# Output projection read by heads, softmax sums on TensorE, and the attention moved ahead of the second FFN product in a decode kernel

## The chip, the cores and the metric

The kernel runs on one core of a Trainium2 chip. A core has five engines that run their own instruction streams and wait for each other through semaphores: TensorE (PE: matmuls and the loads of their stationary operand), VectorE (DVE), ScalarE (ACT), GpSimd (POOL) and SyncE (SP), whose queue issues nearly all of this kernel's DMAs. Sixteen DMA engines move data between HBM and SBUF. The metric is the device time of one execution in microseconds (us); lower is better. Times of several executions are given by their median.

## The reference

One token of a decoder layer, with an attention part and an MLP part in parallel, both from the same normalised row:

```python
xn  = layernorm(x)                                   # x: [1, 1, 1024]
# attention: 32 query heads, 4 KV heads, the last 4096 positions of the cache
q   = (xn @ wq).reshape(1, 1, 32, 128).transpose(0, 2, 1, 3)
s   = einsum("bhqd,bhkd->bhqk", q, repeat(k_cache[:, :, -4096:], 8, axis=1)) * 128**-0.5
o   = einsum("bhqk,bhkd->bhqd", softmax(s), repeat(v_cache[:, :, -4096:], 8, axis=1))
A   = o.transpose(0, 2, 1, 3).reshape(1, 1, 4096) @ wo
# MLP
h   = gelu(layernorm(xn) @ w1 + b1)                  # 3584 wide, tanh form
B   = h @ w2 + b2
out = x + A + B
```

All inputs are bf16. With one token, every weight and every cache row is used once: wq and wo have 8.4 MB each, w1 and w2 7.3 MB each, the window of K and of V 4.2 MB each, 39.9 MB together.

## The kernel before

The program is written in blocks, one for each step and engine; each engine runs its blocks in the order in which they are written, with no planner or scheduler behind it. So the order of TensorE's work is the order of its blocks in the source. Every engine has one semaphore that counts its marked instructions, and a block waits for a count of another engine.

**Loads.** SP issues, in this order, wq in 8 chunks of 1 MB (L166), w1 in 8 chunks (L169), K in 4 (L172), V in 4 (L177). Then it waits until TensorE has finished the w1 product, because w2 is loaded over w1, and issues w2 in 4 chunks of 9, 9, 8 and 2 groups (L642), and after a wait for the wq product, whose buffer WA it takes, wo in 9 chunks of 4 or 2 groups (L650). Each chunk has its own semaphore. In all of them a partition receives one contiguous piece of DRAM; for wo, partition p holds rows 32p to 32p+31, 8 KB in a chunk of four.

**First half.** TensorE makes the row of q = xn·wq (L292, 64 matmuls with one column of xn as stationary operand and 512 columns of wq moving) and of h = y·w1 (L319, 56 matmuls), each as a row on one partition. Short transpositions turn q into QT (head dimension on partitions, L332) and h into columns (L371). K is transposed in 8 units of 16 blocks (L441), which DVE and ACT copy back from PSUM (L456, L468). The GELU of h runs on DVE and ACT (L381 to L404) into GT, a column for each group of 128.

**Second half, in TensorE's order.** Scores: 128 matmuls of 128x8 (L484), one for each KV head and block of 128 positions. The maximum for each head is taken on DVE (L494), transposed and spread over partitions by TensorE (L504, L520), and subtracted on DVE (L546); ACT takes the exp into Pb (L555). While DVE and ACT do this, TensorE adds x and b2 into the output row (4 matmuls, L530 and L534) and the first chunk of w2 (18 matmuls, L413). Then come the sums of the softmax: DVE reduces Pb over the blocks (L560, SUMP), TensorE adds over partitions with a column of ones (L568), DVE takes the reciprocal (L574), TensorE spreads it (L579), DVE copies it to RB. P·V is 128 matmuls of 128x8 (L595). DVE multiplies by RB into OT: head dimension on partitions, one column for each head (L606).

**From OT to wo.** With wo's rows at partition p = row // 32, the column that belongs to wo's group j holds the output values 32p + j, which OT has at another place. So OT is transposed (L612), copied (L618), multiplied by four 0/1 matrices that POOL made at the start in EB (L626), and copied to OJ (L635). The rest of w2 follows (38 matmuls, L413), then 64 matmuls of wo (L667) with a column of OJ as stationary operand. All of x, b2, w2 and wo accumulate in one row of PSUM:

```python
pe.wait_ge(s_wo[j], 16)
...
last = pe.matmul(
    PS[0:1, 6 * 512 + n * 512: 6 * 512 + (n + 1) * 512],
    lhsT=OJ[:, jj:jj + 1],
    rhs=WA[:, jj * D + n * 512: jj * D + (n + 1) * 512],
    start=False, stop=(jj == HQ - 1))
```

ACT and DVE copy the halves of the row to SBUF (L678, L684), and SP stores it (L690).

Of the kernel before, what the change touches and what calls it, by code (L numbers as in the profile page):

```python
# [37 lines left out]
def bass_parallel_sum__sliding_block_cached__mixer_channel_mlp__decode_kernel(  # L38
# [60 lines left out]
    DIAG = nc.alloc_sbuf_tensor("DIAG", [32, 32], dt.float32)  # L99
    NMB = nc.alloc_sbuf_tensor("NMB", [128, 32], dt.float32)  # L100
    Pb = nc.alloc_sbuf_tensor("Pb", [128, HKV * NBLK * REP], dt.bfloat16)
    SUMP = nc.alloc_sbuf_tensor("SUMP", [128, 32], dt.float32)
    REC = nc.alloc_sbuf_tensor("REC", [1, 32], dt.float32)
    RB = nc.alloc_sbuf_tensor("RB", [128, 32], dt.float32)
    OT = nc.alloc_sbuf_tensor("OT", [128, HQ], dt.bfloat16)
    KV = nc.alloc_sbuf_tensor("KV", [128, HKV * W + HKV * NBLK * DH], dt.bfloat16)
    KT = KV[:, 0:HKV * W]
    V = KV[:, HKV * W: HKV * W + HKV * NBLK * DH]
    OTt = nc.alloc_sbuf_tensor("OTt", [32, 128], dt.bfloat16)
    EB = nc.alloc_sbuf_tensor("EB", [32, 4 * 128], dt.bfloat16)  # L110
    OJ = nc.alloc_sbuf_tensor("OJ", [128, 32], dt.bfloat16)
    W1 = nc.alloc_sbuf_tensor("W1", [128, KC * F], dt.bfloat16)
    W2 = W1[:, 0:FC * D]
    WA = nc.alloc_sbuf_tensor("WA", [128, KC * NQ], dt.bfloat16)
# [10 lines left out]
    b2_row = B_b2.rearrange("(o n) -> o n", o=1)  # L125
    b1_T = B_b1.rearrange("(p c) -> p c", c=FC)
    w2_pcn = B_w2.rearrange("(p c) n -> p c n", c=FC)
    wo_pjn = A_wo.rearrange("(p j) n -> p j n", j=32)
    out_row = out.rearrange("b s n -> (b s) n")

    STATE = {}
# [1 line left out]
    with nc.Block() as block:  # L133

        @block.gpsimd
        def _(pool):
            with nc.allow_non_contiguous_dma(reason="small loads"):
                pool.dma_start(X8[:, :], x_rows8).then_inc(s_x8, 16)
                pool.dma_start(XBR[:, 0:D], x_row).then_inc(s_xrow, 16)
                pool.dma_start(XBR[:, D:2 * D], b2_row).then_inc(s_b2, 16)  # L140
                pool.dma_start(B1T[:, :], b1_T).then_inc(s_b1T, 16)
            POOL.mark(pool.memset(identb[:, :], 0.0))
            pool.wait_ge(POOL.sem, POOL.cnt)
            STATE["c_identb"] = POOL.mark(pool.affine_select(
                out=identb[:, :], in_=identb[:, :],
                pattern=[[-1, 128]], compare_op=ALU.not_equal, fill=1.0,
                base=0, channel_multiplier=1))
            POOL.mark(pool.memset(identf[:, :], 0.0))
            pool.wait_ge(POOL.sem, POOL.cnt)
            STATE["c_identf"] = POOL.mark(pool.affine_select(  # L150
                out=identf[:, :], in_=identf[:, :],
                pattern=[[-1, 128]], compare_op=ALU.not_equal, fill=1.0,
                base=0, channel_multiplier=1))
            STATE["c_onesf"] = POOL.mark(pool.memset(onesf[:, :], 1.0))
            POOL.mark(pool.memset(EB[:, :], 0.0))
            pool.wait_ge(POOL.sem, POOL.cnt)
            for r in range(4):
                ins = pool.tensor_copy(
                    EB[:, r * 128:(r + 1) * 128].rearrange("h (a b) -> h a b", b=4)[:, :, r],
                    identb[0:32, 0:32])  # L160
            STATE["c_eb"] = POOL.mark(ins)

        @block.sync
        def _(sp):
# [211 lines left out]
        def gelu_sections():  # L376
            @block.vector
            def _(dve):
                dve.wait_ge(PE.sem, STATE["pe_hT"])
                dve.wait_ge(s_b1T, 16)  # L380
                STATE["d_HT"] = DVE.mark(dve.tensor_tensor(  # L381
                    out=HT[:, :], in0=PSb[:, 7 * 1024: 7 * 1024 + 2 * FC: 2], in1=B1T[:, :], op=ALU.add))
                dve.wait_ge(DVE.sem, DVE.cnt)
                DVE.mark(dve.tensor_tensor(out=U2[:, :], in0=HT[:, :], in1=HT[:, :], op=ALU.mult))
                dve.wait_ge(DVE.sem, DVE.cnt)
                DVE.mark(dve.tensor_scalar(out=U2[:, :], in0=U2[:, :], scalar1=0.044715, scalar2=1.0,
                                           op0=ALU.mult, op1=ALU.add))
                dve.wait_ge(DVE.sem, DVE.cnt)
                STATE["d_T"] = DVE.mark(dve.tensor_tensor(out=U2[:, :], in0=U2[:, :], in1=HT[:, :], op=ALU.mult))
# [29 lines left out]
        for u in range(NUNIT):  # L419
            g = u // 2  # L420
            hu = u % 2
            if u == 3:
                hT_section()

            @block.tensor
            def _(pe, u=u, g=g, hu=hu):
# [35 lines left out]
            if use_act:  # L462
                @block.scalar
                def _(act, u=u, g=g, hu=hu):
# [3 lines left out]
                    STATE["a_ktcopy"][u] = ACT.mark(act.activation(  # L468
                        out=KT[:, g * W + (hu * 16 + 8) * 128: g * W + (hu * 16 + 16) * 128],
                        in_=PSb[:, bk * 1024:(bk + 1) * 1024], func=ACTF.Copy))  # L470

        gelu_sections()

        @block.tensor
        def _(pe):
# [44 lines left out]
            STATE["pe_nmb"] = PE.mark(pe.matmul(  # L520
                PS[:, 2 * 512 + 128: 2 * 512 + 160], lhsT=onesf[0:32, :], rhs=DIAG[:, :]))

        @block.tensor
        def _(pe):
            pe.wait_ge(DVE.sem, STATE["d_QT"])
            pe.wait_ge(DVE.sem, STATE["d_HT"])
            pe.wait_ge(s_xrow, 16)
            pe.wait_ge(s_b2, 16)
            for n in range(2):
                pe.matmul(  # L530
                    PS[0:1, 6 * 512 + n * 512: 6 * 512 + (n + 1) * 512],
                    lhsT=identb[0:1, 0:1], rhs=XBR[0:1, n * 512:(n + 1) * 512],
                    start=True, stop=False)
                pe.matmul(  # L534
                    PS[0:1, 6 * 512 + n * 512: 6 * 512 + (n + 1) * 512],
                    lhsT=identb[0:1, 0:1], rhs=XBR[0:1, D + n * 512:D + (n + 1) * 512],
                    start=False, stop=False)
            pe.wait_ge(DVE.sem, STATE["d_GT"])
            w2_chunk_mms(pe, 0)

        @block.vector
        def _(dve):
            dve.wait_ge(PE.sem, STATE["pe_nmb"])
# [10 lines left out]
            act.wait_ge(DVE.sem, STATE["d_se"])  # L554
            STATE["a_exp"] = ACT.mark(act.activation(out=Pb[:, :], in_=PS[:, 0:1024], func=ACTF.Exp, scale=SCALE))  # L555

        @block.vector
        def _(dve):
            dve.wait_ge(ACT.sem, STATE["a_exp"])
            STATE["d_sump"] = DVE.mark(dve.tensor_reduce(  # L560
                out=SUMP[:, :],
                in_=Pb[:, :].rearrange("p (g b h) -> p g h b", g=HKV, b=NBLK, h=REP),
                axis=AX.X, op=ALU.add))

        @block.tensor
        def _(pe):
            pe.wait_ge(DVE.sem, STATE["d_sump"])
            STATE["pe_tot"] = PE.mark(pe.matmul(  # L568
                PS[0:1, 3 * 512: 3 * 512 + 32], lhsT=onesf[:, 0:1], rhs=SUMP[:, :]))

        @block.vector
        def _(dve):
# [33 lines left out]
            STATE["d_OT"] = DVE.mark(dve.tensor_tensor(  # L606
                out=OT[:, :], in0=PS[:, 4 * 512: 4 * 512 + 32], in1=RB[:, :], op=ALU.mult))

        @block.tensor
        def _(pe):  # L610
            pe.wait_ge(DVE.sem, STATE["d_OT"])
            STATE["pe_ott"] = PE.mark(pe.matmul(  # L612
                PSb[0:32, 5 * 1024: 5 * 1024 + 128], lhsT=OT[:, :], rhs=identb[:, :], is_transpose=True))

        @block.vector
        def _(dve):
            dve.wait_ge(PE.sem, STATE["pe_ott"])
            STATE["d_ott"] = DVE.mark(dve.tensor_copy(OTt[:, :], PSb[0:32, 5 * 1024: 5 * 1024 + 128]))  # L618

        @block.tensor  # L620
        def _(pe):
            pe.wait_ge(DVE.sem, STATE["d_ott"])
            pe.wait_ge(POOL.sem, STATE["c_eb"])
            last = None
            for r in range(4):
                last = pe.matmul(  # L626
                    PS[:, 5 * 512 + 128: 5 * 512 + 160],
                    lhsT=EB[:, r * 128:(r + 1) * 128], rhs=OTt[:, r * 32:(r + 1) * 32],
                    start=(r == 0), stop=(r == 3))
            STATE["pe_oj"] = PE.mark(last)  # L630

        @block.vector
        def _(dve):
            dve.wait_ge(PE.sem, STATE["pe_oj"])
            STATE["d_OJ"] = DVE.mark(dve.tensor_copy(OJ[:, :], PS[:, 5 * 512 + 128: 5 * 512 + 160]))  # L635

        @block.sync
        def _(sp):
            sp.wait_ge(PE.sem, STATE["pe_h"])
            c0 = 0  # L640
            for j, nch in enumerate(W2_CHUNKS):
                sp.dma_start(  # L642
                    W2[:, c0 * D:(c0 + nch) * D].rearrange("p (c n) -> p c n", c=nch),
                    w2_pcn[:, c0:c0 + nch, :],
                ).then_inc(s_w2[j], 16)
                c0 += nch
            sp.wait_ge(PE.sem, STATE["pe_q"])
            j0 = 0
            for j, nj in enumerate(WO_CHUNKS):
                sp.dma_start(  # L650
                    WA[:, j0 * D:(j0 + nj) * D].rearrange("p (jj n) -> p jj n", jj=nj),
                    wo_pjn[:, j0:j0 + nj, :],
                ).then_inc(s_wo[j], 16)
                j0 += nj

        @block.tensor
        def _(pe):
            for j in range(1, len(W2_CHUNKS)):
                w2_chunk_mms(pe, j)
            pe.wait_ge(DVE.sem, STATE["d_OJ"])  # L660
            last = None
            jj = 0
            for j, nj in enumerate(WO_CHUNKS):
                pe.wait_ge(s_wo[j], 16)
                for _ in range(nj):
                    for n in range(2):
                        last = pe.matmul(  # L667
                            PS[0:1, 6 * 512 + n * 512: 6 * 512 + (n + 1) * 512],
                            lhsT=OJ[:, jj:jj + 1],
                            rhs=WA[:, jj * D + n * 512: jj * D + (n + 1) * 512],  # L670
                            start=False, stop=(jj == HQ - 1))
                    jj += 1
            STATE["pe_fin"] = PE.mark(last)

        @block.scalar
# [46 lines left out]
```

## Time and profile before

| what | value |
|---|---|
| median of 6 runs | 111.44 us (109.59 to 111.86) |
| profiled execution, its own time | 111.26 us |
| its span in the profile | 109.1 us |
| PE busy, matmuls | 83.6 us (77%), 705 matmuls |
| DVE, ACT, POOL busy | 22.5, 14.2, 4.6 us |
| DMA | 39.95 MB, mean 366 GB/s over the span |
| chain that ended last | DMA of w1 and w2 46%, PE 34%, SP queue 13% |
| w2 matmuls (L413) | 56, mean 482 ns |
| wo matmuls (L667) | 64, mean 379 ns |
| scores (L484), P·V (L595) | 128 each, 3.4 and 3.5 us |

The span runs from the first to the last instruction of the profiled execution; 2.16 us of its time lie outside it. Matmuls are pipelined, so that the mean duration of one is longer than the distance between two; distances come from the starts. "PEclk" is the clock that TensorE was granted, as a share of full speed. The chain is followed back from the last instruction, at each step to what released it; "issue" in it is time in which an engine waited for nothing that the profile shows. Busy time is an average over stages with different limits, so the stage where a change lies has to be read by itself.

### The profile page before, as it was taken

The page shows a single profiled execution, that of the slowest core. Times are in us where ns is not written, and L with a number is a line of the kernel's source. Part 1 is how long each engine was busy: PE and PEld are TensorE (multiplying, and loading weights), DVE is VectorE, ACT ScalarE, POOL GpSimd, SP SyncE. Part 2 cuts the span into 40 slices and gives each one's busy share as a digit, 9 for nine tenths or more (in the row PEclk, how much of TensorE's full clock was granted, in tenths as well). Part 3 has the DMA queues.
Part 4 walks back from the last instruction along what each step waited for, and adds up shares of the span by engine and source line. Part 5 has one row for each costly group of instructions (what it writes and reads, how often), then busy time and mean ns, then how long its engine had stood idle before and what let it go on. Part 6 is the DMA issues. An engine that isn't in the chain of part 4 may idle for free.

```text
span 109.1 us, 1585 instructions
## 1 busy us (share of the span) xinstructions
PE 83.6 (77%) x705; PEld 41.7 (38%) x705; DVE 22.5 (21%) x49; ACT 14.2 (13%) x16; POOL 4.6 (4%) x18
## 2 busy tenths in 40 slices
PE   0022999999299888499989381998818999999991
PEld 0021233432133222399989230236702334334330
DVE  0015300000700000557396567001001000000002
ACT  4000600000600000534473002000000000000002
POOL 6820000000000000000000000000000000000000
PEclk9999999999999999959999555559965599999999
DMA  3999999999999999999999999999999999970000
GB/s 54 415 420 424 430 418 415 424 421 418 421 415 406 418 426 423 415 421 424 418 412 443 425 419 426 418 461 389 413 418 421 406 421 424 413 302 18 0 0 1
DMA packets 5463, 39.95 MB, mean 366 GB/s; under 512 B 721, under 2 KB 721, under 8 KB 2130
## 3 DMA queue, kind: packets, MB, share of 16 engines
q1 hardware_dynamic: 5330, 39.85, 88.6%
q8 instruction: 5, 0.08, 0.3%
q0 software_dynamic: 128, 0.01, 0.1%
HBM read 39.86 MB, written 0.00 MB: 366 GB/s over the span
## 4 chain that ended last, share of the span: by engine, by line
DMA 46%; PE 34%; SPq 13%; issue 3%; DVE 1%
DMA W<-in_B_w_dram 46%; PE PS L413 16%; PE PS L667 13%; SPq L169 9%; SPq L166 4%; PE PS L595 3%; PE PS L319 2%; DVE ROW L684 1%; PE PS L579 0%; DVE REC L574 0%; PE PS L612 0%; PE PS L626 0%; DVE OTt L618 0%; DVE OT L606 0%; PE PS L568 0%
## 5 line engine op out<-in xcount | busy, mean ns | idle before, releaser
L413 PE MATMUL PS<-W,GT 128*1 128x512 bf16 x56 | 17.2, 482 | 2.2 <-DMA W<-in_B_w_dram 2.2
L292 PE MATMUL PS<-WA,XNTb 128*1 128x512 bf16 x64 | 16.0, 416 | 0.3 <-DVE msy L253 0.3
L319 PE MATMUL PS<-W,YTb 128*1 128x512 bf16 x56 | 12.9, 378 | 3.9 <-DVE ROW L302 2.4
L667 PE MATMUL PS<-WA,OJ 128*1 128x512 bf16 x64 | 14.0, 379 | 0.0
L413 PEld LDWEIGHTS PS<-W,GT 128*1 128x1 bf16 x56 | 5.5, 101 | 13.9 <-issue 10.1
L441 PE MATMUL PS<-identb,KV 128*128 128x128 bf16 x128 | 8.9, 240 | 1.5 <-ACT ROW L345 1.5
L292 PEld LDWEIGHTS PS<-WA,XNTb 128*1 128x1 bf16 x64 | 5.7, 90 | 10.2 <-issue 2.9
L441 PEld LDWEIGHTS PS<-identb,KV 128*128 128x128 bf16 x128 | 8.6, 110 | 1.6 <-ACT ROW L345 1.6
L319 PEld LDWEIGHTS PS<-W,YTb 128*1 128x1 bf16 x56 | 4.3, 83 | 12.5 <-DMA W<-in_B_w_dram 3.5
L667 PEld LDWEIGHTS PS<-WA,OJ 128*1 128x1 bf16 x64 | 5.4, 84 | 8.4
L456 DVE COPY KV<-PS 128x1024 bf16<-128x1024 bf16 x10 | 6.5, 687 | 4.0 <-PE PS L441 4.0
L468 ACT ACTIVATE KV<-PS 128x1024 bf16<-128x1024 bf16 x6 | 5.9, 1021 | 5.9 <-PE PS L441 5.9
L678 ACT ACTIVATE ROW<-PS 1x512 bf16<-1x512 f32 x1 | 0.6, 586 | 40.6 <-PE PS L667 40.6
L684 DVE CAST ROW<-PS 1x512 bf16<-1x512 f32 x1 | 0.7, 679 | 24.0 <-PE PS L667 24.0
L595 PE MATMUL PS<-Pb,KV 128*128 128x8 bf16 x128 | 3.5, 166 | 2.6 <-issue 2.6
L302 DVE CAST ROW<-PS 1x2048 bf16<-1x2048 f32 x1 | 2.3, 2279 | 14.8 <-PE PS L292 14.8
L186 PE MATMUL PS<-identb,X 8*128 8x8 bf16 x1 | 0.2, 185 | 6.7 <-DMA X<-in_A_x_dram 6.7
L595 PEld LDWEIGHTS PS<-Pb,KV 128*128 128x128 bf16 x128 | 3.4, 96 | 2.7 <-issue 2.7
L307 ACT ACTIVATE ROW<-PS 1x2048 bf16<-1x2048 f32 x1 | 1.9, 1866 | 13.8 <-PE PS L292 13.8
L484 PE MATMUL PS<-QT,KV 128*128 128x8 bf16 x128 | 3.4, 167 | 0.3 <-ACT KV L468 0.3
L484 PEld LDWEIGHTS PS<-QT,KV 128*128 128x128 bf16 x128 | 3.4, 98 | 0.5 <-DVE KV L456 0.5
L345 ACT ACTIVATE ROW<-PS 1x1536 bf16<-1x1536 f32 x1 | 1.4, 1439 | 15.8 <-PE PS L332 15.8
(84 smaller groups left out, 37.0 us busy)
## 6 DMA issues: line engine op xcount, KB each, us to landing
WA<-in_A_wq_dram SPq DMA_DIRECT2D x8, 1024.0 KB, 12.0
W<-in_B_w_dram SPq DMA_DIRECT2D x8, 896.0 KB, 25.9
WA<-in_A_wo_dram SPq DMA_DIRECT2D x7, 1024.0 KB, 34.6
W<-in_B_w_dram SPq DMA_DIRECT2D x2, 2304.0 KB, 26.3
KV<-in_A_k_cache_dram SPq DMA_DIRECT2D x4, 1024.0 KB, 26.6
KV<-in_A_v_cache_dram SPq DMA_DIRECT2D x4, 1024.0 KB, 27.4
W<-in_B_w_dram SPq DMA_DIRECT2D x1, 2048.0 KB, 33.3
WA<-in_A_wo_dram SPq DMA_DIRECT2D x2, 512.0 KB, 24.3
```

The lines of the kernel that those rows point to most:

```text
L166: sp.dma_start(WA[:, k * NQ:(k + 1) * NQ], A_wq[k * 128:(k + 1) * 128, :]).then_inc(s_wq[k], 16)
L169: sp.dma_start(W1[:, k * F:(k + 1) * F], B_w1[k * 128:(k + 1) * 128, :]).then_inc(s_w1[k], 16)
L292: last = pe.matmul(PS[0:1, n * 512:(n + 1) * 512], lhsT=XNTb[:, k:k + 1], rhs=WA[:, k * NQ + n * 512: k * NQ + (n + 1) * 512], start=(k == ...
L302: STATE["d_qrow0"] = DVE.mark(dve.tensor_copy(Qrow[:, 0:2048], PS[0:1, 0:2048]))
L319: last = pe.matmul(PS[0:1, (n + 1) * 512:(n + 2) * 512], lhsT=YTb[:, k:k + 1], rhs=W1[:, k * F + n * 512: k * F + (n + 1) * 512], start=(k ...
L413: pe.matmul(PS[0:1, 6 * 512 + n * 512: 6 * 512 + (n + 1) * 512], lhsT=GT[:, c:c + 1], rhs=reg[:, n * 512:(n + 1) * 512], start=False, stop ...
L441: last = pe.matmul(PSb[:, col0: col0 + 128], lhsT=KT[:, g * W + b * 128: g * W + (b + 1) * 128], rhs=identb[:, :], is_transpose=True)
L456: last = dve.tensor_copy(KT[:, g * W + (hu * 16 + 8 * s_) * 128: g * W + (hu * 16 + 8 * s_ + 8) * 128], PSb[:, bk * 1024:(bk + 1) * 1024])
L468: STATE["a_ktcopy"][u] = ACT.mark(act.activation(out=KT[:, g * W + (hu * 16 + 8) * 128: g * W + (hu * 16 + 16) * 128], in_=PSb[:, bk * 102 ...
L484: last = pe.matmul(PS[:, bank_base + b * 8: bank_base + (b + 1) * 8], lhsT=KT[:, g * W + b * 128: g * W + (b + 1) * 128], rhs=QT[:, g * 8: ...
L595: last = pe.matmul(PS[:, 4 * 512 + g * REP: 4 * 512 + (g + 1) * REP], lhsT=V[:, (g * NBLK + b) * DH:(g * NBLK + b + 1) * DH], rhs=Pb[:, (g ...
L667: last = pe.matmul(PS[0:1, 6 * 512 + n * 512: 6 * 512 + (n + 1) * 512], lhsT=OJ[:, jj:jj + 1], rhs=WA[:, jj * D + n * 512: jj * D + (n + 1 ...
```

## The change

It changes four things together.

1. wo is loaded by heads: partition d of group h receives row 128h + d, so that the column of OT for head h is the stationary operand as it is. A chunk of four groups is then four rows of 2 KB for each partition. The transposition, the permutation and their buffers (OTt, EB, OJ) go.
2. The sums of the softmax are made by 128 matmuls with a column of bf16 ones as stationary operand, straight from Pb, in place of DVE's reduction and one fp32 matmul.
3. TensorE's order after the maximum is now: sums, broadcast of the reciprocal, P·V, x and b2, all of w2, wo. Before, x, b2 and the first w2 chunk stood ahead of the sums, and the other w2 chunks behind the permutation.
4. The addition of b1 (HT) is written ahead of the fourth transposition unit, and the rest of the GELU behind the exp.

The diff, cut to its core:

```diff
-    POOL.mark(pool.memset(EB[:, :], 0.0))
-    pool.wait_ge(POOL.sem, POOL.cnt)
-    for r in range(4):
-        ins = pool.tensor_copy(
-            EB[:, r * 128:(r + 1) * 128].rearrange("h (a b) -> h a b", b=4)[:, :, r],
-            identb[0:32, 0:32])
-    STATE["c_eb"] = POOL.mark(ins)
+    STATE["c_onesb"] = POOL.mark(pool.memset(ones_b[:, :], 1.0))
...
         STATE["d_HT"] = DVE.mark(dve.tensor_tensor(...op=ALU.add))
-        dve.wait_ge(DVE.sem, DVE.cnt)
+
+def gelu_sections2():
+    @block.vector
+    def _(dve):
+        dve.wait_ge(DVE.sem, STATE["d_HT"])
         DVE.mark(dve.tensor_tensor(out=U2[:, :], in0=HT[:, :], in1=HT[:, :], op=ALU.mult))
...
     if u == 3:
         hT_section()
+        gelu_sections()
...
-gelu_sections()
-
 ...
...
...
-pe.wait_ge(DVE.sem, STATE["d_GT"])
-w2_chunk_mms(pe, 0)
 ...
-dve.wait_ge(ACT.sem, STATE["a_exp"])
-STATE["d_sump"] = DVE.mark(dve.tensor_reduce(
-    out=SUMP[:, :], in_=Pb[:, :].rearrange("p (g b h) -> p g h b", g=HKV, b=NBLK, h=REP),
-    axis=AX.X, op=ALU.add))
-pe.wait_ge(DVE.sem, STATE["d_sump"])
-STATE["pe_tot"] = PE.mark(pe.matmul(
-    PS[0:1, 3 * 512: 3 * 512 + 32], lhsT=onesf[:, 0:1], rhs=SUMP[:, :]))
+gelu_sections2()
+pe.wait_ge(ACT.sem, STATE["a_exp"])
+pe.wait_ge(POOL.sem, STATE["c_onesb"])
+for g in range(HKV):
+    for b in range(NBLK):
+        last = pe.matmul(
+            PS[0:1, 3 * 512 + g * REP: 3 * 512 + (g + 1) * REP],
+            lhsT=ones_b[:, 0:1],
+            rhs=Pb[:, (g * NBLK + b) * REP:(g * NBLK + b + 1) * REP],
+            start=(b == 0), stop=(b == NBLK - 1))
+STATE["pe_tot"] = PE.mark(last)
 ...
...
...
-wo_pjn = A_wo.rearrange("(p j) n -> p j n", j=32)
 for j, nh in enumerate(WO_CHUNKS):
     sp.dma_start(
-        WA[:, j0 * D:(j0 + nj) * D].rearrange("p (jj n) -> p jj n", jj=nj),
-        wo_pjn[:, j0:j0 + nj, :],
+        WA[:, h0 * D:(h0 + nh) * D].rearrange("p (h n) -> p h n", h=nh),
+        A_wo[h0 * 128:(h0 + nh) * 128, :].rearrange("(h d) n -> d h n", h=nh),
     ).then_inc(s_wo[j], 16)
...
-for j in range(1, len(W2_CHUNKS)):
...
+pe.wait_ge(DVE.sem, STATE["d_GT"])
+for j in range(len(W2_CHUNKS)):
     w2_chunk_mms(pe, j)
-pe.wait_ge(DVE.sem, STATE["d_OJ"])
+pe.wait_ge(DVE.sem, STATE["d_OT"])
 for j, nh in enumerate(WO_CHUNKS):
     pe.wait_ge(s_wo[j], 16)
     for _ in range(nh):
         for n in range(2):
             last = pe.matmul(PS[0:1, 6 * 512 + n * 512: 6 * 512 + (n + 1) * 512],
-                lhsT=OJ[:, jj:jj + 1], rhs=WA[:, jj * D + n * 512: jj * D + (n + 1) * 512],
+                lhsT=OT[:, h:h + 1], rhs=WA[:, h * D + n * 512: h * D + (n + 1) * 512],
                 start=False, stop=(h == HQ - 1))
```

More of the change, by code (lines that the diff above doesn't have):

```diff
@@ L101, in bass_parallel_sum__sliding_block_cached__mixer_channel_mlp__decode_kernel @@
     Pb = nc.alloc_sbuf_tensor("Pb", [128, HKV * NBLK * REP], dt.bfloat16)
-    SUMP = nc.alloc_sbuf_tensor("SUMP", [128, 32], dt.float32)
     REC = nc.alloc_sbuf_tensor("REC", [1, 32], dt.float32)
@@ L108, in bass_parallel_sum__sliding_block_cached__mixer_channel_mlp__decode_kernel @@
     V = KV[:, HKV * W: HKV * W + HKV * NBLK * DH]
-    OTt = nc.alloc_sbuf_tensor("OTt", [32, 128], dt.bfloat16)
-    EB = nc.alloc_sbuf_tensor("EB", [32, 4 * 128], dt.bfloat16)
-    OJ = nc.alloc_sbuf_tensor("OJ", [128, 32], dt.bfloat16)
+    ones_b = nc.alloc_sbuf_tensor("ones_b", [128, 2], dt.bfloat16)
     W1 = nc.alloc_sbuf_tensor("W1", [128, KC * F], dt.bfloat16)
@@ L521, in _ @@
                 PS[:, 2 * 512 + 128: 2 * 512 + 160], lhsT=onesf[0:32, :], rhs=DIAG[:, :]))
[L523 to L537, printed above, removed]
-            pe.wait_ge(DVE.sem, STATE["d_GT"])
-            w2_chunk_mms(pe, 0)
         @block.vector
@@ L555, in _ @@
             STATE["a_exp"] = ACT.mark(act.activation(out=Pb[:, :], in_=PS[:, 0:1024], func=ACTF.Exp, scale=SCALE))
-        @block.vector
-        def _(dve):
-            dve.wait_ge(ACT.sem, STATE["a_exp"])
-            STATE["d_sump"] = DVE.mark(dve.tensor_reduce(
-                out=SUMP[:, :],
-                in_=Pb[:, :].rearrange("p (g b h) -> p g h b", g=HKV, b=NBLK, h=REP),
-                axis=AX.X, op=ALU.add))
+        gelu_sections2()
         @block.tensor
         def _(pe):
-            pe.wait_ge(DVE.sem, STATE["d_sump"])
-            STATE["pe_tot"] = PE.mark(pe.matmul(
-                PS[0:1, 3 * 512: 3 * 512 + 32], lhsT=onesf[:, 0:1], rhs=SUMP[:, :]))
+            pe.wait_ge(ACT.sem, STATE["a_exp"])
+            pe.wait_ge(POOL.sem, STATE["c_onesb"])
+            last = None
+            for g in range(HKV):
[6 more added lines that the diff above has]
+            STATE["pe_tot"] = PE.mark(last)
         @block.vector
@@ L607, in _ @@
                 out=OT[:, :], in0=PS[:, 4 * 512: 4 * 512 + 32], in1=RB[:, :], op=ALU.mult))
[L609 to L635, printed above, removed]
         @block.sync
@@ L647, in _ @@
             sp.wait_ge(PE.sem, STATE["pe_q"])
-            j0 = 0
-            for j, nj in enumerate(WO_CHUNKS):
+            h0 = 0
+            for j, nh in enumerate(WO_CHUNKS):
                 sp.dma_start(
-                    WA[:, j0 * D:(j0 + nj) * D].rearrange("p (jj n) -> p jj n", jj=nj),
-                    wo_pjn[:, j0:j0 + nj, :],
+                    WA[:, h0 * D:(h0 + nh) * D].rearrange("p (h n) -> p h n", h=nh),
+                    A_wo[h0 * 128:(h0 + nh) * 128, :].rearrange("(h d) n -> d h n", h=nh),
                 ).then_inc(s_wo[j], 16)
-                j0 += nj
+                h0 += nh
         @block.tensor
         def _(pe):
-            for j in range(1, len(W2_CHUNKS)):
+            pe.wait_ge(DVE.sem, STATE["d_QT"])
+            pe.wait_ge(DVE.sem, STATE["d_HT"])
+            pe.wait_ge(s_xrow, 16)
+            pe.wait_ge(s_b2, 16)
+            for n in range(2):
+                pe.matmul(
+                    PS[0:1, 6 * 512 + n * 512: 6 * 512 + (n + 1) * 512],
+                    lhsT=identb[0:1, 0:1], rhs=XBR[0:1, n * 512:(n + 1) * 512],
+                    start=True, stop=False)
+                pe.matmul(
+                    PS[0:1, 6 * 512 + n * 512: 6 * 512 + (n + 1) * 512],
+                    lhsT=identb[0:1, 0:1], rhs=XBR[0:1, D + n * 512:D + (n + 1) * 512],
+                    start=False, stop=False)
+            pe.wait_ge(DVE.sem, STATE["d_GT"])
+            for j in range(len(W2_CHUNKS)):
                 w2_chunk_mms(pe, j)
-            pe.wait_ge(DVE.sem, STATE["d_OJ"])
+            pe.wait_ge(DVE.sem, STATE["d_OT"])
             last = None
-            jj = 0
-            for j, nj in enumerate(WO_CHUNKS):
+            h = 0
+            for j, nh in enumerate(WO_CHUNKS):
                 pe.wait_ge(s_wo[j], 16)
-                for _ in range(nj):
+                for _ in range(nh):
                     for n in range(2):
@@ L668, in _ @@
                             PS[0:1, 6 * 512 + n * 512: 6 * 512 + (n + 1) * 512],
[L669 to L672, printed above, removed]
+                            lhsT=OT[:, h:h + 1],
+                            rhs=WA[:, h * D + n * 512: h * D + (n + 1) * 512],
+                            start=False, stop=(h == HQ - 1))
+                    h += 1
             STATE["pe_fin"] = PE.mark(last)
```

## The prediction

> **What bounds the kernel now.** I read the chain that ended last first, because it tells which work was late at each moment, which shares of busy time do not. Its second half (start us, length us, what):
>
> ```profile
> 43.83 23.70 DMA W<-in_B_w_dram
> 67.53 0.14 issue
> 67.67 6.74 PE PS L413 x18
> ...
> 74.90 0.40 PE PS L579 x2
> 75.30 3.27 PE PS L595 x127
> 78.58 2.60 issue
> 81.17 0.20 PE PS L595
> ...
> 82.53 10.42 PE PS L413 x38
> 92.95 13.83 PE PS L667 x64
> 106.78 0.02 issue
> 106.80 0.68 DVE ROW L684
> ```
>
> Until 67.67 us TensorE waits for data (the first chunk of w2). From there to 106.78 us the end is set by TensorE alone: 39 us of its own program order. The loads are done before it: the DMA row of the page falls to 0 at 98.8 us, so the last wo chunk lies in SBUF 8 us before its last matmul. Whatever the change is worth must come out of those 39 us.
>
> Two things in them are slower than they need be. The first is the clock. I cut the span at the moments where the granted clock changes (us, length, PE busy, PEclk, DMA share, GB/s):
>
> ```profile
> 56.07:59.49 3.42, 3.11 (x106) 1.00 1.01 419
> 59.49:62.90 3.41, 1.56 (x46) 0.50 1.10 459
> 66.31:69.73 3.42, 2.06 (x5) 0.50 1.01 431
> 69.73:73.15 3.42, 3.42 (x9) 0.50 0.96 408
> 73.15:76.55 3.40, 2.96 (x62) 1.00 0.94 396
> 79.97:83.38 3.41, 1.61 (x9) 0.50 1.01 420
> 83.38:86.80 3.42, 3.42 (x10) 0.50 1.02 417
> ```
>
> The clock changes on a grid of about 3.41 us. It rises after a whole interval full of 512-wide matmuls (at 73.15 and 86.80), not after one that is 2.06/3.41 = 60% full. So TensorE starts w2 cold twice: 67.67 to 73.15 (5.5 us) and 82.46 to 86.80 (4.3 us). A 512-wide matmul takes 0.427 us apart there, against 13.83/64 = 0.216 us warm, so a cold stretch of w us loses 0.495 w: together 4.9 us.
>
> The second is the 2.60 us "issue" inside L595 (the P·V product), between its 127th and 128th matmul, with nothing to wait for. The DMA view of 78.5 to 81.2 us holds one packet of the instruction queue; in narrow stretches it begins between 78.5 and 78.7:
>
> ```profile
> q8 instruction: 1, 0.02, 2.5%
> ```
>
> TensorE ran out of program. The same view finds the other four instruction packets near 33.5, 53.3, 61.2 and 85.3 us, where TensorE shows no gap. The page has 0.08 MB for 5 packets, 16 KB each.
>
> **The change part by part.** Before 57 us nothing on a critical engine moves: the EB memset and four copies that leave POOL (1.2 us) lay beside the first loads; the HT addition (0.18 us) moves to where DVE waits 1.58 us for transposes. The scores end at 60.66 as before; the maximum, its transposition, the subtraction and the exp end at 66.19 as before, all DVE and ACT. The rest of the GELU (DVE 0.19 + 0.18 + 0.19, ACT 0.23, DVE 0.18 + 0.33 + 0.19 us) now comes after the subtraction that ends at 65.14 and after the exp. With handoffs GT is ready near 67.3; w2 will not ask for it before 75, so 8 us of cover hide it, and without them it would cost 2.2 us. The DVE wait this adds is for ACT's small exp; behind it is queued only the reciprocal of the sums, not due before 69.6. On the SP queue nothing is moved past anything: w2 still waits for pe_h, wo follows. So TensorE can start at 66.2, and I add up its program from there.
>
> *Sums on TensorE.* 128 matmuls, 8 wide with a one-column weight, replace the SUMP reduction (1.95 us, hidden under w2 before) and one fp32 matmul. The nearest rows are L484 (128x8, 3.4 us for 128; the clock fell under it at 59.49, and its matmuls are 25 ns apart before and 26.7 ns after) and L595. 128 x 26.7 ns = 3.4 us, to 69.6. The one-column weight could make it a little shorter (3.2); if a matmul slowed with the clock it would be 6.4. I take 3.4, since L484 hardly noticed the clock.
>
> *Reciprocal and broadcast.* From the end of L568 to the start of L595 it took 74.48 to 75.23; same steps: to 70.35.
>
> *P·V with its instruction fetch.* [...] Stall 1.8 us. P·V ends at 72.8 + 103 x 26.7 ns = 75.55. [...]
>
> *OT, transposition and permutation.* The output matmuls read OT directly: L612, L618, L626 (81.38 to 82.46, 1.1 us) are gone. The OT multiplication (0.19 us) is now hidden by w2. x, b2 and the first w2 chunk move behind P·V; the 1.5 us wait from 66.2 to 67.67 for w2 goes, since by 75.6 three chunks are there and the fourth lands at about 77.6, long before its matmuls. What is late next is TensorE itself.
>
> *Clock.* 60 matmuls of 512 follow in one piece, one cold start instead of two. With this run's grid (76.55, 79.97) the clock rises at 79.97, 4.4 us after 75.55: 10.3 matmuls cold, 49.7 x 0.216 = 10.7 us warm, to 90.65. [...] But in the rows above the clock falls at 59.49 with TensorE 3.11 of 3.42 us "busy" on such 8-wide matmuls. They do not count; I take the row. Other positions of the grid give 2.7 to 6.1 us cold, plus or minus 0.85 us of time.
>
> *wo by heads.* 64 matmuls as before, 14.0 us, to 104.65. The loads change shape: per partition four rows of 2 KB instead of one piece of 8 KB. Packets of 8192 B took 313 ns and of 4096 B 161 ns, which makes 85 ns for 2048 B (the one such packet, the output store, took 86): 4 x 85 = 340 against 313, 1.7 us more over the 8 MB. The last wo chunk lands at 100.5 instead of 98.8; TensorE wants it at 103.6. Hidden by 3 us.
>
> Sum: TensorE ends at 104.65 instead of 106.78, 2.1 us less. The tail (copy, store) stays. The profiled execution has 111.26 us for a span of 109.1, 2.16 outside it: 111.26 - 2.1 = **109.2 us**. The median of the six runs is 111.44, so 2.0% below it.
>
> **The rivals.**
> *The fetch is hidden* (or the small matmuls warm the clock): 1.8 to 2.2 us less, 107.2. For it: four of five packets cost nothing. Against it: the fifth met exactly the pattern that the change doubles.
> [...]
> *wo becomes the bound.* The wo transfer runs from 77.6 (w2 landed) to 98.8, 21.2 us. Four matmuls (0.9 us) follow the last chunk, so it costs nothing against before until it takes 106.8 - 0.9 - 77.6 = 28.3 us, a third longer; at 1.5 times (31.8 us) TensorE ends at 110.3, 114.8 in all. For it: four times as many descriptors from SP. Against it: the 86 ns packet, and an SP issue row of 0.44 us for 128 rows against 0.32 for the single-row store, so some 0.8 for 512, where 2.5 us are to be had.
>
> **How the numbers follow.** One stall 0.55 (109.2; with the grid 108.3 to 110.1, half on each side of 2%), hidden or warm 0.18 (107.2, faster), two stalls 0.15 (112.6, same), wo 0.12 (114.8, mostly slower). Faster by over 2%, about what a measurement of this kernel can tell from no change: 0.27 + 0.18 = 0.45; slower 0.11; the rest 0.44. The range leaves out wo and the lowest of the hidden cases: 107.2 to 112.7; the likeliest case alone has 108.3 to 110.1.
>
> **What would show it.** Sums: 128 matmuls in 3.4 us from 66.2. Fetch: one "issue" of 1 to 2.6 us in P·V near its 26th matmul, none in the sums, an instruction packet a few us before its end. Clock: 0.50 from 59.5 on through all of P·V, one rise 3 to 6 us into w2, then 1.00 to the end. wo: no wait on DMA in its matmuls, last landing near 100. It is wrong if P·V has no gap or two, if w2 starts at 1.00, or if wo matmuls wait for their chunks.

## The result and the profile after

The changed kernel takes 108.09 us (median of 8 runs, 107.19 to 109.33); the kernel before, run beside it, 110.78 us (16 runs, 109.52 to 112.11). The ratio is 0.977 with a 95% interval of 0.971 to 0.983; it is of the fast executions alone, while the medians also count those that ran over 1.5% longer than the fastest of their kernel. The forecast was 109.2 against 111.44, a ratio of 0.980: right in sign and nearly in size. The median lies just under the 108.3 to 110.1 us of the likeliest case and inside the whole range, and the interval still holds the line of 2%.

The profiled execution has 107.85 us for a span of 106.1 us. Its chain from the end of the exp on (start us, length us, what; L542 are the sums, L573 P·V, L408 w2, L631 wo):

```profile
63.73 1.03 ACT Pb L531
...
64.81 3.37 PE PS L542 x128
...
68.60 0.63 PE PS L557 x2
69.23 0.73 PE PS L573 x24
69.96 1.07 issue
71.03 2.94 PE PS L573 x104
...
75.76 14.19 PE PS L408 x56
89.95 13.83 PE PS L631 x64
```

The waits of the permutation and of the first w2 chunk are gone, the sums stand in the chain with 3.37 us, and the "issue" inside P·V is still there: shorter, and behind the 24th matmul instead of the 127th. No wo matmul waits for a load; the last wo packet ends at 100.2 us and TensorE takes the last chunk near 103.

The clock by stretches of the grid (us, length, PE busy, PEclk, DMA share, GB/s):

```profile
66.20:69.60 3.40, 2.96 (x97) 0.50 1.01 428
69.60:73.02 3.42, 2.35 (x88) 0.50 0.97 410
73.02:76.44 3.42, 3.42 (x42) 0.50 0.98 407
76.44:79.85 3.41, 3.41 (x9) 0.51 1.01 385
79.85:83.30 3.45, 3.45 (x17) 1.00 1.05 385
```

One cold start in place of two, and no sign that the 8-wide matmuls warm anything: through sums and P·V (64.81 to 73.97 us) the clock stays at 0.50. No interval was full of them here, because of the reciprocal and the stall; one without a gap comes further down, in the dense version. But the one cold start is 5.9 us long, from the first matmul for x at 73.90 to 79.80.

The two profiles must not be subtracted as they stand. The span is 3.0 us shorter, but 1.4 us of that were won before the scores ended (59.24 against 60.66 us), where the change did nothing: in the profile of before the clock happened to fall to 0.50 for one grid interval (45.84 to 49.26) under the transpositions of K, in this one it did not. First before, then after, over the K transpositions and the transposition of h:

```profile
46.20:57.20 11.00, 10.73 (x156) 0.86 1.01 417
```

```profile
46.20:55.80 9.60, 9.29 (x156) 1.00 1.01 420
```

That this goes with the execution and not with the change is shown by a variant of the changed kernel, the first with the sums on DVE: in its profile the clock from 46 to 57 us, over the same transpositions, averages 0.84, here 1.00, by the same code. So stages are compared below from the end of the exp, E. From E to the last wo matmul TensorE needs 40.6 us before and 39.0 after. The grid lies under this part too: the same first 18 matmuls of w2 take 6.74 us before and 5.97 in the run that follows.

### The profile page after: what moved, and what is told of

Read it like the earlier page. It is cut to its first block, busy times and chain, and to the rows that moved or that the text cites. A ratio compares the mean times of both kernels' runs of the same rounds, so it can differ in the third digit from the quotient of the medians.

```text
span 106.1 us, 1820 instructions
## 1 busy us (share of the span) xinstructions
PE 82.2 (77%) x826; PEld 42.9 (40%) x826; DVE 20.2 (19%) x46; ACT 14.0 (13%) x16; POOL 3.6 (3%) x14
## 4 chain that ended last, share of the span: by engine, by line
PE 50%; DMA 25%; SPq 13%; DVE 4%; ACT 3%; issue 2%
DMA W<-in_B_w_dram 25%; PE PS L408 13%; PE PS L631 13%; SPq L159 10%; PE PS L437 6%; SPq L156 4%; PE PS L573 3%; PE PS L542 3%; PE PS L478 3%; PE PS L361 2%; PE PS L309 2%; ACT ROW L335 1%; DVE PS L522 1%; DVE MXP L488 1%; ACT Pb L531 1%
## 5 line engine op out<-in xcount | busy, mean ns | idle before, releaser
L408 PE MATMUL PS<-W,GT 128*1 128x512 bf16 x56 | 14.3, 422 | 0.0
L631 PE MATMUL PS<-WA,OT 128*1 128x512 bf16 x64 | 14.0, 379 | 0.0
L408 PEld LDWEIGHTS PS<-W,GT 128*1 128x1 bf16 x56 | 5.0, 91 | 9.6 <-issue 3.8
L631 PEld LDWEIGHTS PS<-WA,OT 128*1 128x1 bf16 x64 | 5.4, 84 | 8.4
L437 PE MATMUL PS<-identb,KV 128*128 128x128 bf16 x128 | 7.5, 219 | 1.5 <-ACT ROW L335 1.5
L437 PEld LDWEIGHTS PS<-identb,KV 128*128 128x128 bf16 x128 | 7.2, 98 | 1.6 <-ACT ROW L335 1.6
L642 ACT ACTIVATE ROW<-PS 1x512 bf16<-1x512 f32 x1 | 0.6, 587 | 38.9 <-PE PS L631 38.9
L542 PE MATMUL PS<-Pb,ones_b 128*1 128x8 bf16 x128 | 3.4, 166 | 2.6 <-ACT Pb L531 2.6
L573 PE MATMUL PS<-Pb,KV 128*128 128x8 bf16 x128 | 3.7, 168 | 1.1 <-issue 1.1
L542 PEld LDWEIGHTS PS<-Pb,ones_b 128*1 128x1 bf16 x128 | 3.2, 81 | 2.7 <-ACT Pb L531 2.7
L573 PEld LDWEIGHTS PS<-Pb,KV 128*128 128x128 bf16 x128 | 3.6, 104 | 1.2 <-issue 1.2
```

The lines of the kernel that those rows point to most:

```text
L408: pe.matmul(PS[0:1, 6 * 512 + n * 512: 6 * 512 + (n + 1) * 512], lhsT=GT[:, c:c + 1], rhs=reg[:, n * 512:(n + 1) * 512], start=False, stop ...
L437: last = pe.matmul(PSb[:, col0: col0 + 128], lhsT=KT[:, g * W + b * 128: g * W + (b + 1) * 128], rhs=identb[:, :], is_transpose=True)
L542: last = pe.matmul(PS[0:1, 3 * 512 + g * REP: 3 * 512 + (g + 1) * REP], lhsT=ones_b[:, 0:1], rhs=Pb[:, (g * NBLK + b) * REP:(g * NBLK + b ...
L573: last = pe.matmul(PS[:, 4 * 512 + g * REP: 4 * 512 + (g + 1) * REP], lhsT=V[:, (g * NBLK + b) * DH:(g * NBLK + b + 1) * DH], rhs=Pb[:, (g ...
L631: last = pe.matmul(PS[0:1, 6 * 512 + n * 512: 6 * 512 + (n + 1) * 512], lhsT=OT[:, h:h + 1], rhs=WA[:, h * D + n * 512: h * D + (n + 1) * ...
```

## The experiments

**wo by heads alone.** The kernel before, with the load by heads and without the permutation:

```diff
-    WA[...].rearrange("p (jj n) -> p jj n", jj=nj), wo_pjn[:, j0:j0 + nj, :],
+    WA[...].rearrange("p (h n) -> p h n", h=nh),
+    A_wo[h0 * 128:(h0 + nh) * 128, :].rearrange("(h d) n -> d h n", h=nh),
...
-    # transposition of OT, OTt, four matmuls with EB, OJ
-    lhsT=OJ[:, jj:jj + 1],
+    lhsT=OT[:, jj:jj + 1],
```

> The kernel before with wo loaded by heads alone, without the transposition and permutation of OT; order and sums as before. If that step is worth what its place on TensorE's path says, the 1.1 us between the end of P.V and the next w2 matmul go and nothing else: 110.78 - 1.1 = 109.7 us, a ratio of 0.990. The stall in P.V stays behind its 127th matmul, since only instructions behind it go. The wo loads end near 100.2 instead of 98.8 us and no wo matmul waits. If instead the permutation carries the gain of the whole change, the ratio comes near 0.977. If 2 KB rows cost anything while TensorE is late, the ratio is 1 or above.

Measured: 109.05 us against 110.30, ratio 0.991 (0.986 to 0.995). In the chain, w2 follows P·V at once, and the stall is where it was:

```profile
77.77 2.35 issue
80.12 0.19 PE PS L587
80.31 10.73 PE PS L405 x38
```

The forecast was 0.990. So by time the part that gives the change its name is worth some 1.2 of the 2.7 us, and the rest falls to the other three parts together, by difference. The profiles do not show that rest: from E (66.69) to the last wo matmul (104.87) this run needs 38.2 us, less than the 39.0 of the changed kernel. In part that is the grid: the same first 18 matmuls of w2 took 5.97 us here and 6.74 before. How the gain is shared out between order, sums and GELU is therefore not shown. The last wo packet ended at 100.3 us with nobody waiting for it.

**The permutation kept, but hidden.** The changed kernel with 8 KB pieces, OT's transposition placed behind the first w2 chunk and the permutation behind the second:

```diff
-for j in range(len(W2_CHUNKS)):
-    w2_chunk_mms(pe, j)
+w2_chunk_mms(pe, 0)
+# transposition of OT; DVE copies it to OTt
+w2_chunk_mms(pe, 1)
+# four matmuls with EB; DVE copies the result to OJ
+w2_chunk_mms(pe, 2); w2_chunk_mms(pe, 3)
```

> The changed kernel with wo in 8 KB pieces and the permutation as before, but placed between the w2 chunks: the new order and the new sums without the load by heads. TensorE gets five small matmuls more, 0.4 us, and DVE's copies are hidden under w2, so it should stay within 0.5 us of the changed kernel: a ratio of 0.977 to 0.982. If the load by heads is what pays, it loses the 1.1 us of the permutation: 0.987.

Measured: 108.82 us, ratio 0.985 (0.979 to 0.991). By time this does not decide: the interval overlaps that of the changed kernel (0.971 to 0.983) and holds the rival's 0.987. By the trace it does: the five small matmuls take 0.06 and 0.19 us in the chain, and from E (64.63) to the last wo matmul (103.54) TensorE needs 38.9 us, against 39.0 in the changed kernel. So most of the 1.1 us was the price of matmuls and DVE steps standing alone in the chain one behind the other, each waiting for the one before, and not of the five matmuls.

**Is the stall a block of instructions?** That a block has 256 of them is an assumption of the expectations, and so is what they say of requests. Two runs put extra 8-wide matmuls, which do nothing of use, into the waits for w1 long before. They shift all later instructions in TensorE's stream, by 128 and 40 with the loads counted, and add almost nothing to the path (with 64, the last 8 stand in the chain with 0.18 us):

```diff
     for k in range(KC):
         pe.wait_ge(s_w1[k], 16)
         ...
+        for _ in range(8):          # shift40: 3 for k < 4, else 2
+            pe.matmul(PS[0:1, 0:8], lhsT=YTb[:, 0:1], rhs=YTb[:, 0:8])
```

> The changed kernel with 64 extra 8-wide matmuls (128 instructions) in the waits for w1. If blocks of 256 instructions are what stalls, the boundary behind P.V's 24th matmul moves into the sums, near the 92nd, and is hidden there because its request goes out ahead of the sums; the next one comes to about the 88th matmul of P.V with a request from the 74th sum, and stalls there for about 1.2 us. A stall that has nothing to do with instruction blocks stays behind the 24th.

> The changed kernel with 20 extra 8-wide matmuls (40 instructions, into an unused part of PSUM) spread over the waits for w1, where TensorE is idle. They do no work on the path and only shift where the blocks of 256 instructions end. If entering a block asks for the next and that takes 6 us, the boundary behind P.V's 24th matmul moves to its 4th, the one before it falls ahead of the sums while TensorE waits for the exp, and the request goes out early: the stall in P.V is gone or under 0.3 us, and the next boundary lies in w2, where it is hidden; about 1 us less than the changed kernel, ratio 0.967. If the fetch begins only when TensorE runs dry, the stall moves to the 4th matmul and keeps its 1.1 us or grows to 2.5. If the stall has nothing to do with instruction blocks, it stays behind the 24th matmul.

With 64 matmuls more, the chain reads (L480 scores, L575 P·V):

```profile
55.62 2.52 PE PS L480 x95
58.14 3.48 issue
61.62 1.14 PE PS L480 x33
...
72.74 2.44 PE PS L575 x88
75.18 1.19 issue
76.37 1.23 PE PS L575 x40
```

The stall in P·V is behind the 88th matmul with 1.19 us, as expected to the matmul. I had not counted further back: another stall stands in the scores, behind the 95th, and cost 3.48 us there. From it to the one in P·V there are 254 matmuls, 508 instructions with their loads. The run has 111.06 us, from one execution. With 20 matmuls more:

```profile
69.21 3.50 PE PS L575 x128
...
73.66 0.43 PE PS L615
74.08 1.11 issue
75.20 0.58 PE PS L619
```

P·V is free of it, as expected, but 128 matmuls behind P·V's 4th comes the 4th matmul for x and b2, not w2, and ahead of that one 1.11 us are lost. I had taken x and b2 to last longer than they do. The ratio is 0.982 (0.972 to 0.991), no gain over the changed kernel.

Both runs show that the stall goes with the position in the instruction stream and not with P·V, its data or its semaphores: with the extra matmuls counted, it lies 128 and 127 matmuls behind the place where the changed kernel has it, 256 and 254 instructions with their loads. In P·V they also speak against the rival of a fetch that begins when TensorE runs dry: in the run with 64 no instruction packet lies in 75.1 to 76.4 us, the whole stall there, and in the changed kernel the packet begins at 68.6, 1.4 us before TensorE stops. From the start of the packet to the end of the gap it is 2.4 us in the changed kernel and 2.6 in the kernel before.

The 6 us from entering a block to the arrival of the next are an estimate from one stall, that of the kernel before: from the broadcast, 129 matmuls ahead of it (74.90), to its end (81.17). They do not hold for the stall in the scores: 128 matmuls ahead of it lie near 53.5 us, among the transpositions of K (an estimate from the count and the starts), 8 us before its end at 61.62, and the one instruction packet of 58.1 to 61.7 us lies whole in that stretch, the stall itself. What sets the moment of the packet stays open; no trace shows a request.

**The sums back on DVE.** The changed kernel with the reduction on DVE and one fp32 matmul in place of the 128, at the same place in TensorE's order; then the same with the reciprocal ahead of the rest of the GELU on DVE:

```diff
+# DVE: SUMP <- sum of Pb over the blocks, written ahead of the rest of the GELU
-for g in range(HKV):
-    for b in range(NBLK):
-        last = pe.matmul(PS[0:1, ...], lhsT=ones_b[:, 0:1], rhs=Pb[...], ...)
+pe.matmul(PS[0:1, 3 * 512: 3 * 512 + 32], lhsT=onesf[:, 0:1], rhs=SUMP[:, :])
```

> The changed kernel with the softmax sums taken back to DVE's reduction and one fp32 matmul, at the same place in TensorE's order. My theory: from the end of the exp (E), P.V starts at E + 3.05 instead of E + 4.4 (1.95 us of reduction against 3.4 us of matmuls), and with 254 instructions fewer the instruction block boundary falls behind P.V, so no stall: P.V ends at E + 6.5 instead of E + 9.1, 2.6 us sooner than in the changed kernel. TensorE then ends near the landing of the last wo chunk (100.2 us) plus 0.9 us, so part may be cut off there: 105.5 to 106.5 us, a ratio to the kernel before of 0.952 to 0.961. The rival, that the sums on TensorE are part of the gain because they take DVE out of the path, expects more than the changed kernel has: a ratio over 0.977.

> The version with the sums on DVE, but with the reciprocal written ahead of the rest of the GELU on DVE. In the version before, the reciprocal stood behind the GELU and its wait for ACT: the sums were ready at E + 2.2 us and the reciprocal began at E + 3.6. With it first, P.V starts at E + 3.05 instead of E + 4.5 (E is the end of the exp), 1.4 us sooner, and P.V has no stall: a ratio of 0.960 to 0.965. If the reciprocal is not what P.V waited for, nothing changes against 0.975.

The first came to 0.975 (0.966 to 0.985), well short of the expected 0.952 to 0.961. The chain tells why; the reduction ends at 68.6, but the reciprocal comes at 70.2:

```profile
66.64 1.94 DVE SUMP L537
...
69.98 0.19 DVE GT L400
70.17 0.27 DVE REC L553
...
71.11 3.50 PE PS L574 x128
```

I had left the GELU, with its wait for ACT, between the reduction and the reciprocal, and in the chain it fills the time from 68.59 to 70.17 us. P·V starts at E + 4.5, as late as in the changed kernel, only without a stall. With the reciprocal first it starts at E + 3.4 (expected 3.05; the broadcast took 0.63 us, as in the changed kernel, and not the 0.40 of before):

```profile
65.76 1.95 DVE SUMP L537
...
68.06 0.35 DVE REC L552
...
69.09 3.50 PE PS L575 x128
```

It has 106.63 us beside 110.37, but its four executions spread from 104.35 to 107.13, so the time gives no interval and the expected 0.960 to 0.965 stays undecided. The trace is clearer: P·V ends at E + 6.9, in the changed kernel at E + 9.2. So with the reciprocal where it belongs, 128 tiny matmuls on the path are dearer than the DVE reduction that they replace, by their own time and by the stall that comes with them.

**P·V first.** Nothing in P·V needs the sums; OT does, and OT is needed only for wo. So P·V starts as the exp ends, DVE reduces beside it, and sums and broadcast come later:

```diff
 # TensorE after the exp
+P·V (128 matmuls)
-128 matmuls for the sums; wait for the reciprocal; broadcast
-P·V
+one fp32 matmul on SUMP
 x, b2
+broadcast of the reciprocal
 w2, wo
```

> The changed kernel with the sums on DVE again (reduction and one fp32 matmul) and P.V ahead of them on TensorE: P.V starts as the exp ends, DVE reduces beside it, then the matmul for the sums, x and b2, the broadcast of the reciprocal, w2, wo. If TensorE's own program is all that bounds the changed kernel, P.V ends 3.4 us behind the exp (E) instead of 9.1, w2 ends near E + 19.2 and wo near E + 33.2, that is 98 to 99.4 us. But the last wo chunk lands at 100.2 us and four matmuls follow: so the loads take over as the bound, TensorE ends at 101.1 and the time is 105.2 to 105.5 us, a ratio of 0.955, with a wait on DMA in the wo matmuls. [...] If the loads were not near the bound, it would be 0.93 to 0.94.

Measured: 104.27 us (104.14 to 104.92), ratio 0.948 (0.944 to 0.951): faster than both kernels. The end of its chain:

```profile
83.08 13.29 DMA WA<-in_A_wo_dram
...
96.42 3.63 PE PS L635 x16
```

P·V has no stall, and TensorE catches up with the loads: its wo matmuls now wait for their chunks (1.1 us in all), and the chain leads to a wo transfer. What TensorE would save beyond that cannot be had. The time is even 1 us below the expected. The last wo packet ended at 98.6 us and not at 100.2, and the chunk that TensorE waited for last was not the final one: 16 matmuls follow it, not four.

**What do rows of 2 KB cost once the loads are the bound?**

> The same order as the run with P.V first, but wo in 8 KB pieces as before, with OT's transposition and permutation placed between the first w2 chunks, where DVE's copies are hidden. Where the loads are the bound, 2 KB rows show their price: with 8 KB the last chunk lands at 98.8 us, TensorE ends at 99.7, 1.4 us sooner than with rows of 2 KB: 104 us, a ratio of 0.943. If the permutation costs TensorE what it cost before (1.1 us) or rows of 2 KB cost nothing, it is no faster than the version by heads.

> The version with P.V first, with the broadcast of the reciprocal (two fp32 passes, 0.6 us) moved behind the first w2 chunk, so that x, b2 and w2 stand in one piece. In the run with P.V first the clock stayed at 0.50 for 7.4 us from the first matmul for x, through one grid interval broken by that broadcast. In one piece it should rise 2.7 to 6.1 us after it, on average 1 to 2 us sooner, and TensorE reaches wo sooner by half of that, 0.5 to 1 us. But that version ends with waits on wo loads (last landing at 98.6 us), so little of it is left: 103.6 to 104.2 us, a ratio of 0.940 to 0.947. If the loads are not the bound, 103.3 or less.

> The same with wo in 8 KB pieces, and the transposition and permutation of OT behind the second and third w2 chunks. The traces so far have the last wo chunk at 98.8 to 99.1 us with 8 KB pieces and at 98.6 to 100.3 with rows of 2 KB. So with TensorE off the path the two should now be within 0.5 us of each other: 103.6 to 104.5, a ratio of 0.940 to 0.950. If rows of 2 KB cost the 1.7 us of the packet sum, this one is 1 us or more faster than the one by heads. If the permutation still costs what it did, it is 1 us slower.

The edits move the small steps between the w2 chunks, as in the run with the permutation hidden; "dense" also puts the broadcast behind the first w2 chunk. Ratios: by heads 0.948 (0.944 to 0.951) and dense 0.949 (0.944 to 0.955); with 8 KB 0.953 (0.949 to 0.958) and dense 0.956 (0.951 to 0.962). The expected 1.4 us in favour of 8 KB are not there; the version by heads is 0.7 to 1.0 us ahead by the medians, with intervals that overlap. The test is weaker than it was meant to be: in the profiles of the first 8 KB version and of the dense one by heads E came 2.6 and 2.0 us later than with P·V first, and no wo matmul waited for a load. So what rows of 2 KB cost when every execution is bound by the loads is not shown. The last wo packet ended at 98.6 and 98.8 us by heads and at 99.1 and 98.7 with 8 KB. The packets of 2048 B took 84 ns here, but 88 ns in the changed kernel: from 92 to 94 us the loads ran at 409 GB/s with P·V first and at 387 in the changed kernel. What makes the difference stays open.

Dense brought nothing in time, and it refuted my reason for it: in its profile the clock did not rise at 73.97, although TensorE was busy with 512-wide matmuls through the whole interval before:

```profile
67.15:70.56 3.41, 3.41 (x98) 0.50 0.99 422
70.56:73.97 3.41, 3.41 (x9) 0.50 1.01 427
73.97:77.38 3.41, 3.41 (x9) 0.50 0.95 389
77.38:80.80 3.42, 3.42 (x17) 1.00 1.05 408
```

The first row is an interval without a gap: P·V's small matmuls fill it up to about 69.6 us, x and b2 nearly all of the rest, and the clock does not rise behind it. The first microsecond of the next interval are matmuls for x and b2, whose stationary operand has one row instead of 128. The two runs with the sums on DVE show the same: their clock did not rise at 78.2 and 76.3 us, after intervals with x and b2 in their first half and w2 in the rest, but one interval later. In their chains w2 takes 14.77 and 14.80 us, which makes some 5.4 us cold (an estimate from 0.427 and 0.216 us a matmul). That such one-row matmuls do not count is a reading of these three intervals, not a test.

**The GELU put back.**

```diff
+gelu_sections2()      # ahead of the scores, as before
 # scores, maximum, exp
-gelu_sections2()
```

> The changed kernel with the rest of the GELU back in its place before, ahead of the maximum instead of behind the exp. GT is ready 10 us ahead of its use in both, and DVE waits for the scores where the GELU stood before: no difference to the changed kernel, a ratio of 0.972 to 0.983. If its move mattered (DVE or ACT late for the maximum or the exp), it loses up to 1.4 us: 0.99.

Measured: 107.63 us, ratio 0.978 (0.972 to 0.985). Its move is worth nothing that these runs can tell, as the prediction had it.

## Why the prediction was right

- *That TensorE's own program sets the end, and the loads do not.* Right: no wait for a wo chunk, last packet at 100.2 us where 100.5 was forecast. It holds only as long as TensorE is late: with P·V first, where TensorE ends 36.1 us behind E instead of 39.0, it meets the loads.
- *Sums, 3.4 us.* 3.37 us, 26.3 ns apart at half clock, as the scores' row said.
- *Reciprocal and broadcast, 0.75 us.* About 1.0: the fp32 broadcast took 0.63 us instead of 0.40, at a clock of 0.50. I had taken the row at 1.00.
- *The stall.* Forecast at the 26th matmul of P·V with 1.8 us; found behind the 24th with 1.07 us (0.8 and 1.4 in two variants that have P·V at the same place). The place held: it goes with the count of instructions, as the 128 and 127 matmuls of the two shifts show. No run shows the 1.8 us of the sum, nor the 72.8 at which it lets P·V go on: they were my estimate, from the time of a request for instructions that no trace shows, and the runs have the 0.8 to 1.4 us in their place. The stall was mis-sized by 0.7 us: P·V stopped 0.4 us later behind E than the sum has it, and went on some 0.3 us sooner.
- *The clock.* One cold start, and small matmuls do not warm: right; the clock stayed at 0.50 behind an interval of which P·V filled 2.4 of 3.41 us, with x and b2 behind it (67.15 to 70.56 in the dense version). Its length, 4.4 us in the sum, was 5.9, inside the 2.7 to 6.1 that the prediction allowed: the grid stood differently against E, and the first interval full of wide matmuls began 2.5 us after the first of them. That cost 0.7 us, which the shorter stall gave back by luck.
- *Permutation.* 1.1 us by the sum, 1.25 us by the medians of the run with that part alone (its interval reaches from about 0.5 to 1.5 us). The run with it hidden shows that another cure for the same wait existed.
- *The sum.* From E on it said 38.5 us and the profile has 39.0: 1.6 us gained instead of 2.1. The medians moved by 2.7. Part of the difference is the position of the clock grid, over which two single profiles do not average; how much, the runs do not settle. The 109.2 us were built on a profile in which the transpositions of K ran cold; the profiled changed kernel, where they did not, has 107.85. The steps came as forecast, one by one, but what times the stall is not shown, and that the total came so close is partly luck.
- *The rivals.* A hidden fetch is refuted by the 1.07 us, the case of two stalls by the sums, which have none in their 3.37 us, and wo as the bound by the missing waits. What none of them asked was whether the new order was a good one: the sums need not have been on the path at all.

## What to carry to other kernels

Between two engines, ask of each wait what really needs the value: here the sums were needed 20 us after they were waited for, and moving them off the path gained more, together with the stall that went with them, than the whole change. The long run of tiny matmuls was paid for twice here, with 3.37 us of its own and with the 1.07 us of a stall in P·V that the two runs with the sums on DVE do not have; a stall without a releaser that moves when unrelated instructions are added points here to the instruction stream. And where a clock or another periodic state lies under a stage, compare stages from a common event, not spans.

## What the runs showed of the hardware that was not expected

- Adding 128 instructions that do no work, far ahead of the path, cost 3.5 us in the scores (in one execution) and moved a stall to another place: the position in the instruction stream is a property of the whole program.
- A grid interval of 3.41 us full of 512-wide matmuls did not raise the clock when a part of them had a one-row stationary operand (1.0 of 3.41 us in the dense version). An interval filled by P·V's 8-wide matmuls for most of its length and by x and b2 for the rest did not raise it either.
- Packets of 2048 B took 88 ns in the changed kernel, whose loads ended at 100.2 us, and 84 ns with P·V first, where they ended at 98.6. The cause is open.
